# Attention, gated product and mixture of experts on one core: embedding norms, x scaling, filler banks and planner ranks rearranged

## The chip, the cores and the metric

One core of a Trainium2 chip runs the whole program in one launch. The metric is device time in microseconds (us) of that core; lower is better. The engines are PE (TensorE, matmuls and transposes), DVE (VectorE), ACT (ScalarE), POOL (GpSimd) and SP (SyncE, which here issues DMAs). Each engine works through its own instructions strictly in the order in which they were issued when the program was built.

## The reference

Three stages follow each other, cut here to what matters:

```python
scores = where(causal_mask, -1e9, q @ k.T / 8)        # 2 batches, 12 heads, 448 x 64
attn = exp(scores - max); attn /= attn.sum(-1) + 1e-9
x = (attn @ v) laid out as 896 tokens x 768
x = ((x @ w_a) * (x @ w_b)) @ w_out                   # 768 -> 1536 -> 768, float64 weights
xn = x / (norm(x) + 1e-6); en = expert_emb / (norm(expert_emb) + 1e-6)
expert = argmax(xn @ en.T / tau); gate = softmax(...)[expert]
out = gate * (relu(x @ w1[expert]) @ w2[expert])      # 8 experts, 768 -> 1024 -> 768
```

## The kernel before

**Attention.** Two heads make a pair; there are 12 pairs (6 a batch). A pair has three score units: the last 112 query rows, then the second 112, then the third and first together. Unit by unit, PE makes scores in PSUM (`scores`, L361, and the mask, L367), DVE takes the row extreme (`maxima`, L378), and ACT makes the exponentials (`exps`, L394). These are five sub-blocks of 112 x 448 a pair, 60 in all. Of each sub-block PE makes the transpose (`turn`, L403), ACT evacuates it to half precision (`p_hi`, L406), DVE makes the remainder (`p_lo`, L409), and PE multiplies with v in 12 small matmuls (`pv`, L425 to L427). At the pair's end DVE scales the context into x (`weigh`, L447). Four buffers each hold exponentials and transposed probabilities (NPB, NTB). Ahead of that, a pair's k is scaled by a constant (`k_scale`, L333: on DVE for the first pair, on POOL for the others), and v is scaled and split on POOL (L336, L340, L343). q, k and v come by SP's queue (`load`, L178).

**Between attention and the first product.** After a batch's last pair ACT sums squares of x (`squares`, L474), DVE makes a power of two per row (`norm`, L483 to L488), x is multiplied by it (`x_scale`, L493 on DVE and L495 on ACT), PE transposes it (`turn_x`, L461), and ACT and DVE split it into halves (`x_hi` L464, `x_lo` L468).

**First product.** w_a and w_b arrive as float64, and every 128-wide block is converted by DVE in four operations of 768 elements (`conv_ops`: a L258, b L262, c L266, d L273) with one on ACT (e, L269). A unit (f, hf) is two accumulations of 18 matmuls each (`mm`, L507, 128 x 448), followed by `g_a` (ACT), `g_b` (DVE), `g_hi` (ACT) and `g_lo` (DVE), L511 to L522. There are 24 units, 864 matmuls. Those of batch 0 (hf = 0, f = 0 to 3) may start while attention of batch 1 still runs, and fill PE's free time: they are the fillers. In that stretch PSUM holds two score tiles of two banks, two banks of transposes, one bank of context ("po") and one bank "ac" for the fillers.

**Expert embeddings.** 8 rows of 768 are loaded by POOL's queue (L226) into a part of gE, and DVE makes their norms in a chain of small operations (`emb_tasks`, L290 to L305). PE transposes them (`emb_turn`, L312), and ACT and DVE split them (L318, L321). They are first used in the second half of the first product (`we_mm`).

**What sets the order.** `Plan` is a list scheduler that runs while the program is built. Every operation is recorded with an engine, an estimated cost, what it depends on, and a rank. Among the operations that could start at once on the engine that is free first, the lowest rank is issued. So ranks and estimated costs fix each engine's sequence; on the chip the engines then wait for each other as real durations have it. Conversion n may start after exponentials number C1A + C1B*n (20, 25, ... 55).

Of the kernel before, what the change touches and what calls it, by code (L numbers as in the profile page):

```python
# [85 lines left out]
def fused_kernel(ctx: ExitStack, tc: tile.TileContext, q, k, v, w_a, w_b, w_out, emb, tau, w1, w2, out):  # L86
# [17 lines left out]
    NFIRST, NC1, C1A, C1B = 4, 8, 20, 5  # L104
# [118 lines left out]
    er = gE[:E].rearrange("e f h t -> e (f h t)").bitcast(F32)  # L223
    ej = er[:, DM : 2 * DM]
    er = er[:, :DM]
# [18 lines left out]
    def conv_ops(n, *dest_free, after=None):  # L244
# [45 lines left out]
        lambda: v_.scalar_tensor_tensor(ej, er, 1.0, er, op0=ALU.mult, op1=ALU.mult, accum_out=en),  # L290
# [207 lines left out]
    gt = {}  # L498
# [45 lines left out]
    TIE = {(0, 0): 0.45, (0, 1): 0.45, (1, None): 0.45, (2, 0): 0.45, (2, 1): 0.45}  # L544
# [4 lines left out]
    for pi, (b, hp) in enumerate(pairs):  # L549
# [55 lines left out]
    def unit(f, hf):  # L605
        ops_ = unit_o[f, hf] = []
        for i in range(2):
            for kc in range(KC):
                for n in range(3):
# [4 lines left out]
                    if first_:  # L614
                        deps += last(ac_free, pools["acs"])
# [7 lines left out]
        ac_free.append((gb,))  # L623
        gh = op("ACT", ACTC(S), lambda: g_hi(f, hf), gb, el, rank=501)
# [15 lines left out]
    plan.run([o for x in begun for o in unit_o[x]])  # L640
    prev_mm[0] = mm_o[begun[-1]] if begun else None
# [571 lines left out]
```

## Time and profile before

| | us |
|---|---|
| three runs: median (lowest to highest) | 584.49 (581.29 to 585.14) |
| the profiled execution's own time | 586.54 |
| its span, first to last instruction | 584.7 |
| PE busy in the span | 529.2 (90%) |
| DVE busy | 401.9 (69%) |
| ACT busy | 210.8 (36%) |
| POOL busy | 138.3 (24%) |

A busy share is an average over stages with different limits; the stretches below are read one by one. Matmuls are pipelined, so that a group's time is its end less its start, and the idle time ahead of an instruction stands in square brackets with the engine that ended it.

### The profile page before, as it was taken

What the parts mean: (1) busy time and instruction counts of PE and PEld (TensorE: products, weight loads), DVE (VectorE), ACT (ScalarE), POOL (GpSimd) and SP (SyncE); (2) the same over time, 40 slices, a digit from 0 to 9 for tenths busy, and PEclk for the clock granted to TensorE, in tenths of its full rate; (3) what the DMA queues carried; (4) which work ended last, traced back from release to release, by engine and by line L of the source; (5) the groups of instructions that cost most, each with busy time, mean ns of one, the idle gap of its engine ahead of it and who ended that gap; (6) DMA issues with size and microseconds to landing.
All of it is one profiled execution on the core that took longest, in us unless ns stands there. A gap on an engine that the chain in (4) does not pass through costs nothing. (4 is left out here: it accounts for less than half of the span.)

```text
span 584.7 us, 12576 instructions
## 1 busy us (share of the span) xinstructions
PE 529.2 (90%) x5094; PEld 356.6 (61%) x5094; DVE 401.9 (69%) x628; ACT 210.8 (36%) x487; POOL 138.3 (24%) x134
## 2 busy tenths in 40 slices
PE   0998879998999999999999999967999799999893
PEld 0676667664555555555466666657776768767682
DVE  3589989996799758997314788950989628678000
ACT  0687987894242222433201111122211332223230
POOL 7376655301000000000000000012333434324322
PEclk9999989999999999999999999979999899999998
DMA  6453441133546544698201689829788818756100
GB/s 197 142 164 97 151 144 59 56 109 84 188 131 197 176 143 127 144 261 227 55 1 57 229 286 319 290 84 134 233 251 280 289 49 282 246 196 193 44 15 33
DMA packets 46229, 93.02 MB, mean 159 GB/s; under 512 B 23430, under 2 KB 26502, under 8 KB 46160
## 3 DMA queue, kind: packets, MB, share of 16 engines
q1 hardware_dynamic: 43872, 84.16, 47.9%
q0 software_dynamic: 2288, 7.91, 3.8%
q8 instruction: 47, 0.77, 0.6%
q14 instruction: 22, 0.18, 0.1%
HBM read 79.46 MB, written 9.05 MB: 151 GB/s over the span
## 5 line engine op out<-in xcount | busy, mean ns | idle before, releaser
L507 PE MATMUL ab<-bufA 128*128 128x448 f16 x864 | 168.0, 352 | 2.4 <-ACT asb L511 1.8
L507 PEld LDWEIGHTS <-bufA 128*128 128x128 f16 x864 | 83.3, 98 | 77.5 <-issue 3.1
L893 PE MATMUL x<-woc,gL 128*128 128x512 f16 x336 | 57.9, 327 | 0.0
L983 POOL DMA_INDIRECT x<-xse,gidi x1 | 1.1, 1147 | 234.1 <-DVE bufB L876 234.1
L394 ACT ACTIVATE pr<-sc,mn 112x336 f32<-112x336 f32 (+2 forms) x96 | 46.4, 496 | 18.3 <-DVE mn L378 17.8
L361 PE MATMUL sc<-ld,ld 64*112 64x448 f32 (+3 forms) x192 | 34.8, 463 | 14.5 <-DVE ld L333 14.0
L893 PEld LDWEIGHTS <-gL 128*128 128x128 f16 x336 | 32.2, 98 | 20.6 <-issue 0.2
L1095 PEld LDWEIGHTS <-hh 128*128 128x128 f16 x320 | 30.9, 98 | 20.3 <-issue 0.4
L409 DVE TENSOR_TENSOR tbuf<-pt,tbuf 112x448 f16<-112x448 f32 x60 | 36.1, 618 | 4.6 <-ACT tbuf L406 4.5
L378 DVE TENSOR_REDUCE mn<-sc 112x2 f32<-112x896 f32 (+3 forms) x48 | 34.3, 734 | 5.6 <-PE sc L367 5.5
L1081 POOL TENSOR_TENSOR hl<-hr,hh 128x512 f16<-128x512 f32 x20 | 26.7, 1333 | 46.7 <-ACT hr L1080 38.8
L515 DVE TENSOR_TENSOR asb<-asb,ab 128x448 f32<-128x448 f32 x24 | 14.9, 619 | 32.8 <-PE ab L507 31.5
L406 ACT ACTIVATE tbuf<-pt 112x448 f16<-112x448 f32 x60 | 32.0, 544 | 13.8 <-PE pt L403 13.4
L1098 ACT ACTIVATE y<-py,sc 128x512 f32<-128x512 f32 (+1 forms) x20 | 10.5, 577 | 71.9 <-DMA sc<-xsc,gidi 27.0
L262 DVE SCALAR_TENSOR_TENSOR cv<-raw,cv 128x768 uint32<-128x768 uint32 x36 | 35.6, 989 | 1.1
L403 PE MATMUL pt<-id,pr 112*112 112x112 f32 x240 | 35.2, 273 | 0.1
L872 DVE TENSOR_SCALAR bufC<-rw 128x768 f16<-128x768 f32 (+1 forms) x28 | 20.0, 713 | 21.8 <-DMA rw<-in_moe_w_dram 15.6
L266 DVE SCALAR_TENSOR_TENSOR cv<-raw,cv 128x768 uint32<-128x768 uint32 x36 | 34.3, 952 | 0.5
L427 PE MATMUL po<-vh,tbuf 112*128 112x64 f16 x240 | 27.4, 194 | 7.9 <-DVE tbuf L409 7.9
L876 DVE SCALAR_TENSOR_TENSOR bufC<-rw,bufC 128x768 f16<-128x768 f32 (+1 forms) x28 | 32.6, 1163 | 1.4
L876 DVE SCALAR_TENSOR_TENSOR bufB<-rw,bufB 128x768 f16<-128x768 f32 (+1 forms) x28 | 32.4, 1158 | 1.3
L876 DVE SCALAR_TENSOR_TENSOR bufA<-rw,bufA 128x768 f16<-128x768 f32 (+1 forms) x28 | 30.0, 1073 | 1.3
(223 smaller groups left out, 1274.8 us busy)
## 6 DMA issues: line engine op xcount, KB each, us to landing
rw<-in_moe_w_dram SPq DMA_DIRECT2D x36, 512.0 KB, 5.4
rw<-in_moe_w_dram SPq DMA_DIRECT2D x48, 384.0 KB, 4.3
raw<-in_moe_w_a_dram SPq DMA_DIRECT2D x12, 768.0 KB, 4.3
raw<-in_moe_w_b_dram SPq DMA_DIRECT2D x12, 768.0 KB, 4.4
raw<-in_moe_w_out_dram SPq DMA_DIRECT2D x12, 768.0 KB, 5.1
ld<-in_k_dram SPq DMA_DIRECT2D x12, 224.0 KB, 2.8
ld<-in_q_dram SPq DMA_DIRECT2D x12, 224.0 KB, 3.5
ld<-in_v_dram SPq DMA_DIRECT2D x12, 224.0 KB, 3.5
```

The costliest lines, as they stand in the source:

```text
L262: nc.vector.scalar_tensor_tensor(t, r()[:, :, 1], 0xC0000000, t, op0=ALU.bitwise_and, op1=ALU.bitwise_or)
L266: nc.vector.scalar_tensor_tensor(t, r()[:, :, 0], 29, t, op0=ALU.logical_shift_right, op1=ALU.bitwise_or)
L361: nc.tensor.matmul(sc[:CP, j, o : o + W], qt[hd, c * CP : W], kt[hd, :W], start=n == 0, stop=False)
L378: nc.vector.tensor_reduce(mns[pi][:, c, :], sc[:CP, :, o : o + W], axis=AX.X, op=ALU.min)
L394: nc.scalar.activation(pr[:, d : d + W], sc[:CP, jj, o : o + W], AF.Exp, bias=mn[:, c, jj : jj + 1], scale=-1.0, accum_out=sums[pi][:, c, ...
L403: nc.tensor.transpose(pt[:CP, cs], prs[g][:, cs], id32[:CP, :CP])
L406: nc.scalar.activation(tbufs[g % NTB][:, 0, :S], pts[g][:CP, :S], AF.Copy)
L409: nc.vector.tensor_tensor(tbufs[g % NTB][:, 1, :S], pts.pop(g)[:CP, :S], tbufs[g % NTB][:, 0, :S], op=ALU.subtract)
L507: nc.tensor.matmul(gt[i][:, :S], w[:, h, i, kc, :], x[:, kc, ts], start=kc == n == 0, stop=kc == KC - 1 and n == 2)
L876: nc.vector.scalar_tensor_tensor(dl, R.pop(("raw", j, pc))[:, :n], SE, dh, op0=ALU.mult, op1=ALU.subtract)
L893: nc.tensor.matmul(xp[:, ns], G(f)[:, a, tk], woc[:, f, l, ns], start=st, stop=sp)
L1095: nc.tensor.matmul(py[:, ns], a[:, f, :], w_[:, f, ns], start=st, stop=sp)
```

## The change

1. The embeddings are loaded into x00, a tile used only much later, and their DVE, PE and ACT operations are recorded after attention with rank 400; the squares are written to a part of gL that is free until the end of the first product.
2. All four `x_scale` of a batch run on ACT.
3. The second accumulation of the filler units f = 1 to 3 goes to the bank "po", which is free after the last pair's `weigh`; the first stays in "ac".
4. The planner's ranks are new. Transposes and `p_hi` are drawn ahead of their sub-block (T and H), `pv` is put back (V), the units' scores are drawn apart (S), x transposes are drawn ahead (X). Conversion n may start after exponentials number 10 + 13n, at most the last (59).

```diff
-    NFIRST, NC1, C1A, C1B = 4, 8, 20, 5
+    NFIRST, NC1 = 4, 8
+    RK = dict(S=(-2.0, 5.0, -1.0), M=-1.2, T=-8.1, H=-6.8, L=0.0, V=2.7, sq=5.4, X=-9.5, C1A=10, C1B=13.0)
...
-    er = gE[:E].rearrange("e f h t -> e (f h t)").bitcast(F32)
-    ej = er[:, DM : 2 * DM]
-    er = er[:, :DM]
+    er = x00[:E]
     nc.gpsimd.dma_start(er, emb)
...
-        pte["t"] = pt = acc("pte")
+        pte["t"] = pt = small("pte")
...
-        if c % 2:
-            nc.vector.tensor_scalar(x0, x0, r2[b][:, c : c + 1], None, op0=ALU.mult)
-        else:
-            nc.scalar.activation(x0, x0, AF.Copy, scale=r2[b][:, c : c + 1])
+        nc.scalar.activation(x0, x0, AF.Copy, scale=r2[b][:, c : c + 1])
...
-            gt[i] = acc(f"ab{f}{i}{hf}")
+            gt[i] = psA.tile([P, 512], F32, tag="po", name=f"ab{f}{i}{hf}", bufs=1) if (f, hf, i) in on_po else acc(f"ab{f}{i}{hf}")
...
-    emb_o = None
-    for i, fn in enumerate(emb_tasks):
-        emb_o = op("DVE", 0.2, fn, emb_o, rank=12 + 0.01 * i)
-    eo = op("PE", 0.5, emb_turn, emb_o, rank=13)
-    eh = op("ACT", 0.3, emb_hi, eo, rank=13)
-    el = op("DVE", 0.25, emb_lo, eh, rank=13)
-    ac_free.append((el,))
...
-                t_o[g] = op("PE", 0.4, lambda g=g: turn(g), e_o[g], l_o.get(g - 2), rank=g + 0.5)
+                t_o[g] = op("PE", 0.4, lambda g=g: turn(g), e_o[g], l_o.get(g - 2), rank=g + RK["T"])
...
-        conv_ops(n, after=e_o[C1A + C1B * n])
+        conv_ops(n, after=e_o[min(int(RK["C1A"] + RK["C1B"] * n), NU - 1)])
+    po_free = [(wg_o[len(pairs) - 1],)]
     for f in range(NFIRST):
+        if f >= 1:
+            on_po.add((f, 0, 1))
         unit(f, 0)
...
+    eo = None
+    for i, fn in enumerate(emb_tasks):
+        eo = op("DVE", 1.7 if i == 0 else 0.18, fn, eo, rank=400)
+    eo = op("PE", 0.5, emb_turn, eo, rank=400)
+    eh = op("ACT", 0.3, emb_hi, eo, rank=400)
+    el = op("DVE", 0.25, emb_lo, eh, rank=400)
```

Three places show what moves. The changed kernel's lines stand one to four lower than those of the kernel before.

DVE at the program's start, before: the end of the embedding chain (esm holds its 8 norms, gE the embeddings), the first pair's k (ld), then the first row extremes (mn).

```order
L297 RECIPROCAL esm<-esm 8x1
L298 TENSOR_SCALAR esm<-esm 8x1
L299 TENSOR_SCALAR esm<-esm 8x1
L302 TENSOR_SCALAR esm<-esm 8x1
L303 RECIPROCAL esm<-esm 8x1
L333 TENSOR_SCALAR ld_0_84<-ld_0_84 128x448
L304 TENSOR_SCALAR gE<-gE,esm 8x768
L305 RECIPROCAL rtau<-rtau 128x1
L378 TENSOR_REDUCE mn_174<-sc_159 112x2
L378 TENSOR_REDUCE mn_174<-sc_169 112x2
```

The same place in the changed kernel, from DVE's first instruction:

```order
L188 CAST idb<-id_90 112x112
L190 CAST id_97<-id_90 128x128
L332 TENSOR_SCALAR ld_0_84<-ld_0_84 128x448
L377 TENSOR_REDUCE mn_157<-sc_142 112x2
L377 TENSOR_REDUCE mn_157<-sc_152 112x2
L408 TENSOR_TENSOR tbuf_107<-pt_173,tbuf_107 112x448
L377 TENSOR_REDUCE mn_157<-sc_186 112x2 x2
L408 TENSOR_TENSOR tbuf_109<-pt_181,tbuf_109 112x448
```

The first pair's k is the third instruction now; the embedding chain has gone from here.

DVE around batch 0's `norm` (n0sq), before: cv1 and cv2 are conversions 1 and 2, x0_0 is batch 0's x, tbuf the transposed probabilities.

```order
L409 TENSOR_TENSOR tbuf1_109<-pt29_1083,tbuf1_109 112x448
L266 SCALAR_TENSOR_TENSOR cv1_928<-raw1_263,cv1_928 128x768
L447 TENSOR_TENSOR x0_0_395<-po5_1016,rr5_1088 112x4x128
L258 TENSOR_SCALAR cv2_1150<-raw2_324 128x768
L262 SCALAR_TENSOR_TENSOR cv2_1150<-raw2_324,cv2_1150 128x768
L378 TENSOR_REDUCE mn6_1014<-sc62_1141 112x2 x2
L483 TENSOR_TENSOR n0sq_75<-nsq0_133 112x4
...
L488 TENSOR_SCALAR n0sq_75<-n0sq_75 112x4
L493 TENSOR_SCALAR x0_0_395<-x0_0_395,r20_135 112x768 x2
L409 TENSOR_TENSOR tbuf2_111<-pt30_1127,tbuf2_111 112x448
```

The same place in the changed kernel:

```order
L377 TENSOR_REDUCE mn6_999<-sc61_1037 112x2
L408 TENSOR_TENSOR tbuf1_109<-pt29_1045,tbuf1_109 112x448
L408 TENSOR_TENSOR tbuf2_111<-pt30_1071,tbuf2_111 112x448
L446 TENSOR_TENSOR x0_0_374<-po5_1001,rr5_1069 112x4x128
L482 TENSOR_TENSOR n0sq_75<-nsq0_133 112x4
...
L487 TENSOR_SCALAR n0sq_75<-n0sq_75 112x4
L408 TENSOR_TENSOR tbuf3_113<-pt31_1142,tbuf3_113 112x448
L377 TENSOR_REDUCE mn6_999<-sc62_1147 112x2 x2
```

The conversions have gone from around the norm, and sub-block 30's remainder stands ahead of it instead of behind it.

ACT behind the last pair, before: squares (junk), conversions (bufA from cv), x_scale of batch 1 (x0_1) and its evacuations (px).

```order
L474 ACTIVATE junk_132,nsq1_134<-x0_1_1358 112x640 x2
L518 ACTIVATE gE_79<-asb00_1927 128x448
L269 ACTIVATE bufA_74<-cv5_2030 128x768
L474 ACTIVATE junk_132,nsq1_134<-x0_1_1358 112x128 x4
L511 ACTIVATE asb10_2144<-ab100_2099 128x448
L269 ACTIVATE bufA_74<-cv6_2103 128x768
L495 ACTIVATE x0_1_1358<-x0_1_1358,r21_136 112x768 x2
L464 ACTIVATE bufA_74<-px10_2174 128x448 x2
```

The same place in the changed kernel:

```order
L473 ACTIVATE junk_132,nsq1_134<-x0_1_1294 112x640 x3
L514 ACTIVATE gE_79<-asb00_1854 128x448
L268 ACTIVATE bufA_74<-cv4_2031 128x768
L473 ACTIVATE junk_132,nsq1_134<-x0_1_1294 112x128 x4
L507 ACTIVATE asb10_2118<-ab100_2080 128x448
L491 ACTIVATE x0_1_1294<-x0_1_1294,r21_136 112x768 x4
L268 ACTIVATE bufA_74<-cv5_2104 128x768
L514 ACTIVATE gE_79<-asb10_2118 128x448
L463 ACTIVATE bufA_74<-px10_2155 128x448 x2
```

Four x_scale stand where two stood, and one conversion has moved behind them.

Counted in the two sequences of PE: ahead of the last `pv` matmul stand 39 filler matmuls before and 36 now; between it and the first x transpose of batch 1 stand 29 before and 42 now. The embeddings' transposes stand in the first product now, 41 filler matmuls behind the end of unit (2, 0). Counted in the two sequences of DVE: ahead of the last `weigh` (and behind the embedding chain) stand 7 conversion operations a, 7 b, 6 c and 5 d before, and 5, 5, 5 and 4 now; of conversion 0, a, b and c stand in the third and fourth pair now, in the fifth and sixth before.

## Rows read from the trace of the kernel before

**Rows 1.** Windows: stretch, length, busy us (instructions) of five engines, TensorE clock, DMA share, GB/s.

```profile
core 0: us, PE busy (x) PEld busy (x) DVE busy (x) ACT busy (x) POOL busy (x), PEclk, DMA share, GB/s
13.95:45.00 31.05, 30.11 (x349) 21.20 (x350) 21.77 (x38) 21.68 (x73) 16.99 (x18) 1.00 0.47 145
45.00:127.60 82.60, 74.72 (x976) 54.56 (x975) 79.58 (x136) 71.14 (x220) 40.28 (x37) 0.98 0.34 106
127.60:143.30 15.70, 12.57 (x77) 7.27 (x75) 13.34 (x25) 9.67 (x22) 2.18 (x2) 1.00 0.32 71
143.30:297.00 153.70, 151.82 (x928) 79.84 (x926) 115.60 (x157) 45.78 (x71) 0.00 (x0) 1.00 0.56 159
72.00:84.00 12.00, 8.74 (x106) 6.99 (x105) 10.42 (x23) 9.92 (x28) 4.49 (x3) 0.86 0.46 165
```

**Rows 2.** Timeline of the start: start us, duration us, engine, instruction [idle before, releaser].

```profile
0.81 0.40 SPq L178 DMA_DIRECT2D ld<-in_k_dram  x1
1.27 0.42 SPq L178 DMA_DIRECT2D ld<-in_q_dram  x1
...
9.03 1.70 DVE L290 SCALAR_TENSOR_TENSOR gE<-gE 8x768 f32<-8x768 f32 x1 [7.27 <-DMA gE<-in_moe_expert_emb_dram]
...
9.90 2.03 POOL L333 TENSOR_SCALAR ld<-ld 128x448 f32<-128x448 f32 x1
...
13.53 0.36 DVE L333 TENSOR_SCALAR ld<-ld 128x448 f32<-128x448 f32 x1
13.95 1.84 PE L361 MATMUL sc<-ld,ld 64*112 64x448 f32 x4 [13.95 <-DVE ld L333]
14.70 0.14 DVE L305 RECIPROCAL rtau<-rtau 128x1 f32<-128x1 f32 x1
17.47 0.80 PE L312 MATMUL pte<-id,gE 8*128 8x8 f32 x6
22.19 1.33 PE L361 MATMUL sc<-ld,ld 64*112 64x448 f32 x4
```

**Rows 3.** DMA issues of the first pair's k and q: KB, us from issue to landing.

```profile
ld<-in_k_dram SPq DMA_DIRECT2D x1, 224.0 KB, 2.7
ld<-in_q_dram SPq DMA_DIRECT2D x1, 224.0 KB, 2.8
```

**Rows 4.** Groups by line, DVE, 45 to 127.6 us: count, busy us, mean ns, idle before.

```profile
L262 DVE SCALAR_TENSOR_TENSOR cv<-raw,cv 128x768 uint32<-128x768 uint32 x7 | 7.8, 1117 | 0.2
L266 DVE SCALAR_TENSOR_TENSOR cv<-raw,cv 128x768 uint32<-128x768 uint32 x6 | 5.6, 936 | 0.0
L273 DVE SCALAR_TENSOR_TENSOR bufA<-cv,bufA 128x768 f16<-128x768 f32 x5 | 5.4, 1089 | 0.0
L258 DVE TENSOR_SCALAR cv<-raw 128x768 uint32<-128x768 uint32 x7 | 3.8, 541 | 0.0
L493 DVE TENSOR_SCALAR x<-x,r 112x768 f32<-112x768 f32 x2 | 1.1, 613 | 0.0
```

**Rows 5.** The same view, ACT, the same stretch: x_scale on ACT.

```profile
L495 ACT ACTIVATE x<-x,r 112x768 f32<-112x768 f32 x2 | 1.8, 928 | 0.0
```

**Rows 6.** Timeline around batch 0's norm: DVE's conversion b, POOL's v_lo, PE's pv.

```profile
70.59 1.80 DVE L262 SCALAR_TENSOR_TENSOR cv<-raw,cv 128x768 uint32<-128x768 uint32 x1
...
70.04 1.53 POOL L343 TENSOR_TENSOR vl<-ld,vh 112x512 f16<-112x512 f32 x1
...
75.98 0.20 PE L427 MATMUL po<-vh,tbuf 112*128 112x64 f16 x1 [3.26 <-DVE tbuf L409]
```

**Rows 7.** Waits, 45 to 127.6 us: who waited for whom, us in total, times, longest.

```profile
ACT tbuf L406 <- PE pt L403: 8.2, 11, 1.5
...
PE po L427 <- DVE tbuf L409: 7.1, 9, 3.3
```

**Rows 8.** Timeline of PE behind the last pair (fillers and x transposes).

```profile
126.68 3.00 PE L507 MATMUL ab<-bufA 128*128 128x448 f16 x15
130.59 2.81 PE L507 MATMUL ab<-bufA 128*128 128x448 f16 x14 [0.90 <-ACT asb L511]
133.23 1.70 PE L461 MATMUL px<-id,x 112*128 112x112 f32 x16
...
136.51 0.95 PE L461 MATMUL px<-id,x 112*128 112x112 f32 x8 [0.82 <-DVE bufA L468]
```

More of the change, by code (lines that the diff above doesn't have):

```diff
@@ L560, in fused_kernel @@
         vl_o[pi] = op("POOL", 1.2, lambda pi=pi: v_lo(pi), vh, rank=r0)
-        for u, rk in ((0, -3), (1, -1), (2, 1)):
+        for u, rk in enumerate(RK["S"]):
             sc_o[pi, u] = so = op("PE", SCOST[u], lambda pi=pi, u=u: scores(pi, u), k_o[pi], ld_[pi, 0],
                                   *last(sc_free, 2), rank=r0 + rk)
-            mx[pi, u] = op("DVE", 0.08 * len(UNITS[u]) + 0.00104 * 2 * W_(u), lambda pi=pi, u=u: maxima(pi, u), so, rank=r0 + rk)
+            mx[pi, u] = op("DVE", 0.08 * len(UNITS[u]) + 0.00104 * 2 * W_(u), lambda pi=pi, u=u: maxima(pi, u), so, rank=r0 + rk + RK["M"])
             mine = []
@@ L571, in fused_kernel @@
                 mine.append(e_o[g])
-                t_o[g] = op("PE", 0.4, lambda g=g: turn(g), e_o[g], l_o.get(g - 2), rank=g + 0.5)
-                h = op("ACT", ACTC(S), lambda g=g: p_hi(g), t_o[g], v_o.get(g - NTB), rank=g + 0.6)
-                l_o[g] = op("DVE", DVEC(S), lambda g=g: p_lo(g), h, rank=g + 0.6)
-                v_o[g] = op("PE", 0.37, lambda g=g: pv(g), l_o[g], vl_o[pi], wg_o.get(pi - 1), v_o.get(g - 1), rank=g + 1.5)
+                t_o[g] = op("PE", 0.4, lambda g=g: turn(g), e_o[g], l_o.get(g - 2), rank=g + RK["T"])
+                h = op("ACT", ACTC(S), lambda g=g: p_hi(g), t_o[g], v_o.get(g - NTB), rank=g + RK["H"])
+                l_o[g] = op("DVE", DVEC(S), lambda g=g: p_lo(g), h, rank=g + RK["L"])
+                v_o[g] = op("PE", 0.37, lambda g=g: pv(g), l_o[g], vl_o[pi], wg_o.get(pi - 1), v_o.get(g - 1), rank=g + RK["V"])
             sc_free.append(mine)
@@ L584, in fused_kernel @@
             sq_o[b, part, c] = op("ACT", ACTC(LATE if not part else DM - LATE) + 0.2, lambda b=b, c=c, part=part: squares(b, c, part),
-                                  wg_o[pi], rank=r0 + NSB + 5 - 6 * part)
+                                  wg_o[pi], rank=r0 + NSB + RK["sq"] - (RK["sq"] + 1) * part)
         if part == 0:
@@ L588, in fused_kernel @@
         no = op("DVE", 0.7, lambda b=b: norm(b), *(o for k, o in sq_o.items() if k[0] == b), rank=r0 + NSB)
-        xs_ = [op(("ACT", "DVE")[c % 2], (0.85, 0.6)[c % 2], lambda b=b, c=c: x_scale(b, c), no, rank=r0 + NSB + 0.1 * c) for c in range(NCH)]
+        xs_ = [op("ACT", 0.85, lambda b=b, c=c: x_scale(b, c), no, rank=r0 + NSB + 0.1 * c) for c in range(NCH)]
         for kc in range(KC):
             fr = last(ac_free, 1) if b == 0 else last(sc_free, 2) if kc % 2 == 0 else ()
-            to = op("PE", 0.4, lambda b=b, kc=kc: turn_x(b, kc), *xs_, *fr, x_o.get((b, kc - 1, "t")), rank=r0 + NSB + 3 + 0.1 * kc)
-            ho = op("ACT", ACTC(S), lambda b=b, kc=kc: x_hi(b, kc), to, rank=r0 + NSB + 3 + 0.1 * kc)
-            x_o[b, kc] = lo = op("DVE", DVEC(S), lambda b=b, kc=kc: x_lo(b, kc), ho, rank=r0 + NSB + 3 + 0.1 * kc)
+            to = op("PE", 0.4, lambda b=b, kc=kc: turn_x(b, kc), *xs_, *fr, x_o.get((b, kc - 1, "t")), rank=r0 + NSB + RK["X"] + 0.1 * kc)
+            ho = op("ACT", ACTC(S), lambda b=b, kc=kc: x_hi(b, kc), to, rank=r0 + NSB + RK["X"] + 0.1 * kc)
+            x_o[b, kc] = lo = op("DVE", DVEC(S), lambda b=b, kc=kc: x_lo(b, kc), ho, rank=r0 + NSB + RK["X"] + 0.1 * kc)
             x_o[b, kc, "t"] = to
@@ L614, in unit @@
                     if first_:
-                        deps += last(ac_free, pools["acs"])
+                        deps += last(po_free if (f, hf, i) in on_po else ac_free, pools["acs"])
                     prev_mm[0] = op("PE", 0.189, lambda f=f, hf=hf, i=i, kc=kc, n=n: mm(f, hf, i, kc, n), *deps, rank=5000)
@@ L622, in unit @@
         gb = op("DVE", DVEC(S), lambda: g_b(f, hf), prev_mm[0], ga, rank=500)
-        ac_free.append((gb,))
-        gh = op("ACT", ACTC(S), lambda: g_hi(f, hf), gb, el, rank=501)
+        (po_free if (f, hf, 1) in on_po else ac_free).append((gb,))
+        gh = op("ACT", ACTC(S), lambda: g_hi(f, hf), gb, rank=501)
         gl = op("DVE", DVEC(S), lambda: g_lo(f, hf), gh, rank=501)
@@ L640, in fused_kernel @@
     plan.run([o for x in begun for o in unit_o[x]])
+    on_po.clear()
     prev_mm[0] = mm_o[begun[-1]] if begun else None
```

7 lines of the change are left out of this document (3 added, 4 removed).

## Prediction

> **What bounds the kernel now.** I read the windows of the profile first, by stage [rows 1]. The reader is to see three different limits. Up to 13.95 us PE does nothing. From 45 to 127.6 us, most of attention, DVE is busy for 79.58 of 82.60 us (96%), ACT for 71.14 (86%) and PE for 74.72, so DVE sets the pace there; from 13.95 to 45 us DVE has 9.3 us to spare (21.77 of 31.05). From 143.3 to 297 us, the first product, PE is busy for 151.82 of 153.70 us, and DVE has 38 us to spare (115.60). What follows 297 us is not touched by the change and merely comes earlier or later. So a microsecond of DVE's work is worth most in attention and nothing in the first product, and the total is this: when PE gets its steady stream of first-product matmuls, less those already done as fillers.
>
> The start I read in the timeline [rows 2]. k and q of the first pair are issued at 0.81 and 1.27 us and land 2.7 and 2.8 us later [rows 3], so at 3.5 and 4.1 us. DVE, however, stands at the embeddings' first operation until 9.03 us, because their load lands only then (7.27 us of idle time, released by that DMA). The first pair's k_scale is queued behind the chain and runs at 13.53 us. PE's first score matmul follows at 13.95 us, released by it.
>
> **The change part by part.** The sum is made against the profiled execution, 586.54 us (span 584.7 and 1.8 around it). It lies 2.05 us above the median of the three runs; I carry the difference over to the median, 584.49.
>
> Start. In the changed order k_scale is DVE's third instruction. It needs 0.36 us from 3.5 us on; PE then waits for q, and begins at about 4.2 us instead of 13.95: 9.8 us gained. What is late next is POOL, which scales the second pair's k at 9.90 to 11.93 us [rows 2]. The second pair's scores came 8.2 us after the first pair's (22.19 less 13.95), so they would now be due at 12.4 us, after POOL is done. Bounds: 9.8 us if that margin of 0.5 us holds, nothing if POOL's chain sets the pace of the first pairs (a rival below). I take 9.8.
>
> DVE's load in attention. By the counts of the two sequences, two operations a, two b, one c and one d of the conversions leave attention: 2 x 0.541 + 2 x 1.117 + 0.936 + 1.089 = 5.3 us [rows 4]. Two x_scale of batch 0 go to ACT: 2 x 0.613 = 1.2 us less [rows 4]. And a, b, c of conversion 0 (2.6 us) move from the DVE-bound stretch into earlier pairs, where DVE had 9.3 us to spare. Together 9.1 us leave a stretch in which DVE had 3 us of idle time. They reappear in the first product, under 38 us of DVE's spare time, and cost nothing there; if that cover were gone, PE would wait for weights. Not all 9.1 us can be had: ACT gets two more x_scale (2 x 0.928 us [rows 5]), 73 us of work, and in 82.6 - 9.1 = 73.5 us it would have to be busy without a gap, while it now waits 8.2 us in that stretch for PE's transposes [rows 7]. Bounds 0 and 9.1; I take 5.0, a little over half, which leaves ACT at 94% in 77.6 us.
>
> At batch 0's norm the price can be seen. DVE has conversions ahead of and around the norm, one of them 1.80 us long instead of the mean 1.12 [rows 4, 6], and PE stands 3.26 us at a context matmul for DVE's remainder [rows 6]. That wait is part of the same 9.1 us and isn't counted again. The long one ran while POOL's v_lo took 1.53 us. The Trainium skill (SBUF — State Buffer, Who interferes with whom) says that a DVE instruction with two SBUF inputs and a GpSimd instruction that reads SBUF exclude each other for a whole instruction. The trace agrees with that at this place. It speaks against one edit: conversion 0, moved into earlier pairs, now meets POOL's work for the next pairs. By the rule three such blocks of up to 1 us could be added there and the gain be 12 us; by the row POOL is busy for 17 of 31 us in that stretch [rows 1] and can take them, and the sum stays as it is.
>
> Ranks. Transposes come further ahead of their context matmuls, so that p_hi and p_lo have longer before PE needs them. PE waited for DVE's remainder 7.1 us in nine places, ACT for transposes 8.2 us in eleven [rows 7]. In a stretch that DVE bounds these waits are its shadow; I count nothing, with bounds of 3 us either way (about half of either wait).
>
> Behind the last pair. Before, PE was busy 12.57 of 15.70 us [rows 1], 3.1 us of waits, such as 0.90 us for ACT to empty the single filler bank [rows 8]. With two banks those waits go. But x transposes of batch 1 come later: they began 6.55 us after the last context matmul (133.23 less 126.68 [rows 8]), and with four x_scale in a row on ACT instead of two beside two on DVE they need 2 x 0.928 = 1.9 us more, 8.4 us. PE has 42 fillers ahead of them instead of 29; at 0.19 us each (14 in 2.81 us, the last one's own 0.35 us taken off [rows 8]) that is 8.0 us, so 0.4 us stay uncovered. With some 0.7 us at the next group, 1.1 us of waits are left of 3.1: 2.0 us gained (bounds: 0 and 3.1).
>
> Fillers. 36 instead of 39 are done ahead of the last context matmul: 3 x 0.19 = 0.6 us lost.
>
> Embeddings. Their 0.80 us on PE [rows 2] now stand in the PE-bound product: 0.8 us lost at most. PE comes to them 41 x 0.19 = 7.8 us after the end of unit (2, 0). Behind that end DVE does g_b, a conversion d and g_lo (some 2.3 us) and the chain, 14.84 - 9.03 - 0.36 = 5.45 us [rows 2]: 7.8 us too. PE's wait is therefore between 0 and 1.5 us; I take 0.2, and 1.0 us for all.
>
> Sum: 9.8 + 5.0 + 2.0 - 0.6 - 1.0 = 15.2 us. The profiled execution would take 571.3 us, the median 569.3.
>
> **The rivals.** (a) Only the head is gained. ACT and PE, at 86% and 90% of the stretch already [rows 1], take over as soon as DVE is relieved, and the order's waits stay: 9.8 + 1.0 - 0.6 - 1.0 = 9.2 us, 575.3. For it: 73 us of ACT work cannot shrink. Against it: ACT's 86% contain 8.2 us of waits for PE, which itself waited for DVE.
>
> (b) Everything gives. The stretch loses all of 9.1 us, the tail all of 3.1, and the half-speed time at batch 0 goes too: from 72 to 84 us the granted clock is 0.86 [rows 1], which is 12 x 0.14 = 1.7 us of matmul time, and it follows the 3.26 us wait. The Trainium skill (TensorE: Matmul & The Clock Gate, Part 1) says that the slow clock is the default and activity releases it; the trace agrees, the low value standing at the longest wait of the stretch. Gain 9.8 + 9.1 + 3.1 + 1.7 - 0.6 - 0.8 = 22.3 us, 562.2. Against it: three engines would have to run without gaps together.
>
> (c) The change doesn't do at the start what it says: POOL, which scales k and splits v for the pairs to come, sets the pace of the first pairs, and the 9.8 us come back as waits for POOL. Gain 5.4 us, 579.1. For it: the margin of 0.5 us. Against it: POOL is busy 55% of 13.95 to 45 us.
>
> (d) Slower. Transposes drawn ahead stand in front of ready context matmuls, and PE, strictly in order, waits at each for ACT's exponentials, while ACT waits for PE. Such a wait took 8.2 / 11 = 0.75 us. At all 44 places of the stretch instead of 11 it would cost 33 x 0.75 = 25 us more, and the time would be 584.5 - 15.2 + 25 = 594. It decides from some 20 places more on. Against it: four buffers of exponentials let ACT run ahead of PE.
>
> **How the numbers follow.** The forecast, 566 to 573 us, has a chance of 0.56; (a) 0.18, (b) 0.15, (c) 0.07, (d) 0.04. About 1% is what a measurement of this kernel can tell from no change (its three runs span 0.7%), so faster means below 578.6 us: forecast, (a) and (b), 0.89. (c) lies within 1%: 0.07. Slower: 0.04. The range runs from 562 to 578 us; it leaves out (c), (d) and half of (b), 0.19 together.
>
> **What would show it.** The first score matmul at 4.2 us instead of 13.95, and the second pair's scores near 12.4 us (later, released by POOL: (c)). The last weigh at about 112.8 us instead of 127.6 (9.8 and 5.0 earlier): near 118 it is (a), near 109 (b). No wait of 3 us of PE at batch 0's norm. In the ten microseconds behind the last context matmul at most 1.5 us of PE waits, none of them for ACT's asb. The embeddings' transposes without a wait above 1.5 us. The first product as dense as before from its start on; PE waiting there for conversions would show that DVE's spare time was not where I put it. The forecast is wrong if the last weigh moves by less than 10 or more than 20 us, or if the stage behind 297 us changes its length.

## The result and the profile after

The changed kernel took 569.74 us (median of four runs, 563.65 to 573.23), the kernel before 584.80; the ratio is 0.9675 with a 95% interval of 0.960 to 0.975. Timed again later it took 566.93 us (565.66 to 568.14) against 584.08, ratio 0.9704 (0.967 to 0.974). The forecast was 569.3. Two of the four runs, the profiled one among them, are slow (573.07 and 573.23 us, over 1.5% above the fastest) and are left out of the ratio, which compares the other two (563.65 and 566.40) with the kernel before.

The profiled execution took 573.07 us (span 571.4). Its windows, with the columns of [rows 1]:

```profile
core 0: us, PE busy (x) PEld busy (x) DVE busy (x) ACT busy (x) POOL busy (x), PEclk, DMA share, GB/s
4.20:35.00 30.80, 28.39 (x329) 20.15 (x330) 22.20 (x38) 21.51 (x73) 23.04 (x23) 1.00 0.69 217
35.00:113.00 78.00, 72.83 (x961) 54.60 (x959) 68.98 (x123) 69.56 (x216) 36.04 (x38) 0.96 0.30 95
113.00:130.00 17.00, 16.73 (x121) 9.95 (x120) 16.04 (x29) 13.20 (x29) 1.91 (x2) 1.00 0.52 98
130.00:282.00 152.00, 149.78 (x919) 78.83 (x918) 120.79 (x178) 46.70 (x73) 0.00 (x0) 1.00 0.58 166
```

The stretch that was 45 to 127.6 us in [rows 1] is now 35 to 113 us, 4.6 us shorter; DVE is busy 88% of it instead of 96%, and behind the last pair PE hardly waits (16.73 of 17.00 us). The first product is as dense as before. The timeline of the start, to be held against [rows 2]:

```profile
3.47 0.40 DVE L332 TENSOR_SCALAR ld<-ld 128x448 f32<-128x448 f32 x1 [1.72 <-DMA ld<-in_k_dram]
4.13 1.84 PE L360 MATMUL sc<-ld,ld 64*112 64x448 f32 x4 [4.13 <-DMA ld<-in_q_dram]
...
9.45 1.33 POOL L332 TENSOR_SCALAR ld<-ld 128x448 f32<-128x448 f32 x1
...
12.06 1.01 PE L360 MATMUL sc<-ld,ld 64*112 64x448 f32 x4
```

The first scores wait for q alone, and POOL has the second pair's k ready at 10.78 us, 1.3 us ahead of its use. PE behind the last pair, to be held against [rows 8]:

```profile
113.81 8.11 PE L503 MATMUL ab<-bufA 128*128 128x448 f16 x42
121.75 1.70 PE L460 MATMUL px<-id,x 112*128 112x112 f32 x16
123.29 1.49 PE L503 MATMUL ab<-bufA 128*128 128x448 f16 x7
125.03 0.96 PE L460 MATMUL px<-id,x 112*128 112x112 f32 x8 [0.26 <-DVE bufA L467]
125.83 12.27 PE L503 MATMUL ab<-bufA 128*128 128x448 f16 x64
138.35 0.53 PE L311 MATMUL pte<-id,x 8*128 8x8 f32 x6 [0.25 <-DVE x L303]
```

42 fillers run without a gap up to the x transposes, no wait is for asb, and the embeddings' transposes cost 0.53 us and a wait of 0.25. The waits of attention (35.3 to 114.5 us), for [rows 7]:

```profile
ACT tbuf L405 <- PE pt L402: 3.6, 7, 0.9
...
PE po L426 <- DVE tbuf L408: 1.3, 1, 1.3
```

ACT's wait for transposes fell from 8.2 to 3.6 us, PE's for remainders from 7.1 to 1.3. The largest stall that is left is batch 0's join (56 to 72 us). There ACT makes six squares in a row, then four x_scale in two runs, and PE waits for the exponentials behind the squares:

```profile
59.14 0.31 ACT L473 ACTIVATE junk<-x 112x128 bf16<-112x128 f32 x1
...
60.21 0.99 PE L402 MATMUL pt<-id,pr 112*112 112x112 f32 x4 [2.07 <-ACT pr L393]
...
61.69 1.75 ACT L491 ACTIVATE x<-x,r 112x768 f32<-112x768 f32 x2
...
64.75 1.75 ACT L491 ACTIVATE x<-x,r 112x768 f32<-112x768 f32 x2
```

```profile
56.00:72.00 16.00, 11.50 (x123) 8.10 (x122) 7.87 (x19) 13.91 (x41) 6.01 (x6) 0.79 0.26 87
```

DVE is busy for half of these 16 us, ACT for 13.91, and PE's granted clock is 0.79. Before, DVE held the corresponding place [rows 6].

### The profile page after: what moved, and what is told of

It reads as the page before. It is cut to its first block, busy times and chain, and to the rows that moved or that the text cites. A ratio compares the mean times of both kernels' runs of the same rounds, so it can differ in the third digit from the quotient of the medians.

```text
span 571.4 us, 12592 instructions
## 1 busy us (share of the span) xinstructions
PE 527.4 (92%) x5094; PEld 357.4 (63%) x5094; DVE 396.5 (69%) x624; ACT 213.5 (37%) x491; POOL 130.7 (23%) x134
## 5 line engine op out<-in xcount | busy, mean ns | idle before, releaser
L393 ACT ACTIVATE pr<-sc,mn 112x336 f32<-112x336 f32 (+2 forms) x96 | 46.7, 500 | 12.4 <-DVE mn L377 12.4
L1079 POOL TENSOR_TENSOR hl<-hr,hh 128x512 f16<-128x512 f32 x20 | 25.5, 1274 | 50.5 <-ACT hr L1078 42.2
L874 DVE SCALAR_TENSOR_TENSOR bufA<-rw,bufA 128x768 f16<-128x768 f32 (+1 forms) x28 | 31.5, 1124 | 1.3
L511 DVE TENSOR_TENSOR asb<-asb,ab 128x448 f32<-128x448 f32 x24 | 14.8, 618 | 25.1 <-PE ab L503 24.9
L1077 ACT ACTIVATE hh<-ph 128x512 f16<-128x512 f32 x20 | 12.0, 599 | 49.7 <-PE ph L1071 49.6
```

The lines of the kernel that those rows point to most:

```text
L393: nc.scalar.activation(pr[:, d : d + W], sc[:CP, jj, o : o + W], AF.Exp, bias=mn[:, c, jj : jj + 1], scale=-1.0, accum_out=sums[pi][:, c, ...
L874: nc.vector.scalar_tensor_tensor(dl, R.pop(("raw", j, pc))[:, :n], SE, dh, op0=ALU.mult, op1=ALU.subtract)
```

## The experiments

All times of a stage are from the one profiled execution of each kernel; "first scores" and "last weigh" are starts; "fillers" are those ahead of the last context matmul; there is no E8; "behind" is from the product's end to the end of the span. Times and ratios come from four series, each with its own runs of the kernel before (median 584.54 us for E1 to E4; 584.08 for the changed kernel again, E5, E6 and E9; 584.68 for E7, E10 and E11; 585.18 for E12), and these alone differ by 1.1 us.

| kernel | first scores | last weigh | fillers | product's end | behind | median (lowest to highest) | ratio to before (95%) |
|---|---|---|---|---|---|---|---|
| before | 13.95 | 127.62 | 39 | 295.03 | 289.7 | 584.49 (581.29 to 585.14) | |
| changed | 4.13 | 114.54 | 36 | 280.35 | 291.0 | 569.74 (563.65 to 573.23) | 0.9675 (0.960 to 0.975) |
| changed, again | 4.21 | 113.47 | 36 | 279.16 | 285.0 | 566.93 (565.66 to 568.14) | 0.9704 (0.967 to 0.974) |
| E1 part 1 alone | 4.16 | 119.18 | 39 | 287.49 | 287.6 | 574.81 (573.26 to 576.82) | 0.9807 (0.975 to 0.986) |
| E2 part 1 undone | 13.39 | 121.76 | 36 | 287.71 | 288.4 | 577.03 (575.50 to 577.89) | 0.9845 (0.979 to 0.990) |
| E3 part 2 undone | 4.08 | 109.76 | 18 | 287.62 | 285.6 | 574.91 (574.86 to 578.04) | 0.9835 (0.977 to 0.990) |
| E4 part 3 undone | 4.06 | 114.71 | 36 | 282.34 | 287.1 | 569.24 (567.44 to 571.10) | 0.9710 (0.965 to 0.977) |
| E5 parts 1 to 3 | 4.19 | 121.59 | 49 | 284.71 | 285.1 | 572.07 (570.53 to 576.11) | 0.9798 (0.976 to 0.984) |
| E6 old conversion times alone | 4.13 | 113.19 | 36 | 278.21 | 287.7 | 567.36 (565.72 to 567.98) | 0.9703 (0.967 to 0.974) |
| E7 ranks T, H, L, V alone | 4.19 | 113.69 | 36 | 283.67 | 289.0 | 574.54 (574.18 to 584.88) | 0.9865 (0.981 to 0.992) |
| E9 old ranks, new conversion times | 5.00 | 119.61 | 46 | 284.71 | 287.6 | 572.03 (569.99 to 574.98) | 0.9791 (0.975 to 0.983) |
| E10 = E3 + second bank for all | 4.18 | 109.57 | 18 | 288.79 | 286.8 | 575.15 (570.38 to 577.30) | 0.9825 (0.977 to 0.988) |
| E11 join spread | 4.04 | 112.77 | 18 | 284.98 | 287.5 | 572.92 (571.24 to 574.25) | 0.9806 (0.977 to 0.985) |
| E12 = E10 + old conversion times | 4.86 | 113.35 | 18 | 284.88 | 286.9 | 573.98 (571.55 to 576.55) | 0.9799 (0.975 to 0.985) |

The stage behind the product differs between two executions of the changed kernel itself by 6 us, with the same work in it:

```profile
280.40:571.30 290.90, 261.22 (x2784) 194.73 (x2782) 168.64 (x258) 61.78 (x102) 66.23 (x53) 0.97 0.57 176
```

```profile
279.20:564.00 284.80, 257.81 (x2784) 191.31 (x2782) 168.34 (x258) 61.64 (x102) 66.98 (x53) 0.99 0.58 180
```

The granted clock is 0.97 in the one and 0.99 in the other. So the parts are compared by the product's end, and totals by medians. What was expected of the repetition:

> The changed kernel unaltered, once more, so that the variants beside it have a measure on the same chip. Expected: 569.7 us (563 to 573), last weigh at 114.5 us, the first product's end at 280.4, and the stage behind it 287 to 291 us long, which is where its own executions differ from each other.

**E1 and E2: the start.** E1 is the kernel before with the embeddings' lines of the change; E2 is the changed kernel without them. Two of those lines:

```diff
+    er = x00[:E]
...
+        eo = op("DVE", 1.7 if i == 0 else 0.18, fn, eo, rank=400)
```

> Only part 1 of the change, put into the kernel before: the embedding norms leave the start, everything else (order, ranks, banks, x_scale) stays. Theory: the start is worth its full 9.8 us less about 1.0 us for the embeddings' transposes in the first product, so the time is about 9 us (1.5%) below the kernel before, ratio 0.985; first score matmul at 4.1 us instead of 13.95 and the last weigh near 118 instead of 127.6. Rival 1 (POOL sets the pace of the first pairs): first score matmul at 4.1 us, but the last weigh only 3 to 6 us earlier, ratio 0.990 to 0.995. Rival 2 (all of the change's gain is the head, the rest is nothing): ratio 0.974, as the whole change has it.

> The changed kernel with part 1 undone: the embedding chain is back at the start, parts 2 to 4 stay. Theory: the parts are independent, so what is left is 13.1 less 9.8 = 3.3 us in attention and some 1.5 us behind it: first score matmul near 14 us, last weigh near 124.4, ratio to the kernel before 0.991 to 0.994 (579.5 to 581.5). Rival (the new ranks need the early start, or bring nothing without it): ratio 1.000 or above, last weigh at 127 or later.

E1 is 9.7 us faster than before (584.54 beside it), E2 7.5 us; together 17.2, which is what the whole change gives when it is timed again, in the next series (584.08 less 566.93). So the two halves add up, and both rivals of E1 fall. E2's last weigh came 5.9 us earlier, more than expected; 0.6 of that is an earlier first score. In E1 the 9.8 us of the first score had become 8.4 at the last weigh: the lead was 9.45 us at the first pair's weigh, 9.1 at the third's, 8.4 at the seventh's, behind the join.

**E3 and E10: x_scale split again.** E3 undoes part 2:

```diff
-        nc.scalar.activation(x0, x0, AF.Copy, scale=r2[b][:, c : c + 1])
+        if c % 2:
+            nc.vector.tensor_scalar(x0, x0, r2[b][:, c : c + 1], None, op0=ALU.mult)
+        else:
+            nc.scalar.activation(x0, x0, AF.Copy, scale=r2[b][:, c : c + 1])
...
+        xs_ = [op(("ACT", "DVE")[c % 2], (0.85, 0.6)[c % 2], lambda b=b, c=c: x_scale(b, c), no, rank=r0 + NSB + 0.1 * c) for c in range(NCH)]
```

> The changed kernel with part 2 undone: x_scale split between ACT and DVE again. In the changed kernel DVE is busy 88% and ACT 89% of attention, and at batch 0's join (pairs 6 to 8) ACT works without a gap at squares and x_scale while PE waits. Theory A (ACT bounds that join and the four x_scale lengthen it): last weigh 1 to 2 us earlier than 114.5, x transposes of batch 1 begin 6.5 us behind the last context matmul instead of 8.15, first product at most 0.4 us earlier for that since fillers cover it; time 0.5 to 2 us below the changed kernel (ratio to it 0.996 to 0.999). Theory B (DVE still bounds): last weigh 1 us later, ratio to the changed kernel 1.001 to 1.003.

Both theories missed. The last weigh came 4.8 us earlier, but the planner now put 18 fillers ahead of it instead of 36 (18 x 0.19 = 3.4 us of PE's time), and behind it the product took far longer. Two rows of the timeline, and the window around the first:

```profile
112.98 6.21 PE L506 MATMUL ab<-bufA 128*128 128x448 f16 x17 [3.48 <-ACT asb L510]
119.03 1.70 PE L460 MATMUL px<-id,x 112*128 112x112 f32 x16
```

```profile
109.00:119.00 10.00, 6.48 (x27) 2.90 (x28) 8.80 (x16) 6.86 (x18) 1.19 (x1) 0.66 0.48 158
```

With 18 fillers done, the next accumulation is due just where ACT makes squares, and asb stands behind seven of them (not nine, as I wrote for E10). PE waits 3.48 us, and the 17 matmuls behind that wait take 6.21 us instead of 3.4, at a granted clock of 0.66. E10 takes that wait away:

```diff
-        if f >= 1:
+        if f >= 0:
             on_po.add((f, 0, 1))
```

> The variant with x_scale split between ACT and DVE, which took 574.9 us, with one thing more: unit (0, 0)'s second accumulation goes to the bank po too, so that no filler behind the last context matmul needs ACT to have emptied ac. In the split variant PE stood 3.48 us there for asb, which ACT could make only behind nine squares, and the 17 fillers behind that wait took 6.21 us instead of 3.3. Theory (that wait and the half clock behind it made the split variant slow, not the split): the wait goes, the last weigh stays at 109.8 us, the product ends at 279 to 282 instead of 287.6, the time is 565 to 569. Rival (fewer fillers ahead, 18 instead of 36, make it slow): the product still ends at 285 or later, time 572 or more.

The wait went (1.00 us for the last weigh is left there, at full clock behind it), and the product still ended at 288.8 us. A later wait took its place:

```profile
110.31 5.65 PE L506 MATMUL ab<-bufA 128*128 128x448 f16 x29 [1.00 <-DVE x L446]
...
130.92 0.53 PE L311 MATMUL pte<-id,x 8*128 8x8 f32 x6 [0.48 <-DVE x L303]
134.77 0.55 PE L506 MATMUL ab<-bufA 128*128 128x448 f16 x2 [3.32 <-ACT bufA L268]
136.23 14.01 PE L506 MATMUL ab<-bufA 128*128 128x448 f16 x58 [0.90 <-DVE bufA L272]
```

```profile
135.00:142.00 7.00, 6.10 (x18) 2.41 (x17) 6.89 (x10) 0.84 (x1) 0.00 (x0) 0.52 0.69 238
```

A conversion isn't ready when the fourth unit needs it, and nearly 7 us at the lower of the two clocks follow, 1.2 GHz (0.52 of full speed granted). My rival (fewer fillers) gave the right time, but not by its own mechanism. On DVE that conversion's b and c stand right behind the embeddings' chain, which runs from 126.42 to 130.93 us:

```profile
126.42 0.94 DVE L289 SCALAR_TENSOR_TENSOR gL<-x 8x768 f32<-8x768 f32 x1
...
130.79 0.14 DVE L304 RECIPROCAL rtau<-rtau 128x1 f32<-128x1 f32 x1
...
131.38 0.94 DVE L261 SCALAR_TENSOR_TENSOR cv<-raw,cv 128x768 uint32<-128x768 uint32 x1
...
132.90 0.94 DVE L265 SCALAR_TENSOR_TENSOR cv<-raw,cv 128x768 uint32<-128x768 uint32 x1
```

**E12: is that the conversions put off, or the embeddings' chain?** E10 with the old times of the conversions:

```diff
-    ... C1A=10, C1B=13.0)
+    ... C1A=20, C1B=5.0)
```

> The variant with the split x_scale and two banks for all second accumulations (575.2 us, the first product's end at 288.8 us in its profile) with the old times of the conversions (number n after exponentials 20 + 5n) as its only edit. That variant had the last weigh at 109.6 us, but PE stood 3.32 us in the product for a conversion's ACT part at 134.8 us and 0.9 us for its DVE part, and ran at half clock behind it (granted clock 0.52 from 135 to 142 us); when attention ended it had done 4, 4, 4 and 3 of the four DVE operations of the conversions, and this order has 6, 6, 5 and 4. Theory D (conversions that are put off from attention are a debt on DVE, due when the first units of batch 0 need them): the wait at 134.8 us and the half clock behind it go, the last weigh is at 109.5 to 111.5 us, the product ends at 280 to 283 us, the time is 566 to 570 us. Rival E (the embeddings' 4.5 us chain on DVE, which stands ahead of that conversion, is what PE waits for): a wait of 2 to 4 us stays within 10 us of the embeddings' transposes, the product ends at 285 us or later, the time is 572 us or more.

```profile
117.00:145.00 28.00, 28.00 (x164) 15.63 (x163) 25.73 (x53) 10.06 (x18) 2.17 (x2) 1.00 0.40 126
```

PE worked without any gap from 117 to 145 us at full clock, with the embeddings' chain still on DVE (131.0 to 135.5 us): as theory D said, the wait goes when the conversions come earlier, and the chain by itself doesn't make it. That the chain had no part in E10's wait isn't shown: its 4.5 us stood right ahead of the late conversion there, and the two waits are 4.2 us together; no run took it away. The product still ended at 284.9 us instead of 280 to 283. The last weigh moved from 109.6 to 113.4 us, with 18.9 us of DVE's conversions ahead of it instead of 12.7, and PE then waited for it, with the lower clock behind (26 matmuls at full clock take some 5.1 us):

```profile
114.09 6.56 PE L506 MATMUL ab<-bufA 128*128 128x448 f16 x26 [1.59 <-DVE x L446]
```

The time stayed (ratio to E10, which is of another series, 0.999, 0.994 to 1.005), as rival E had it, though not by its mechanism. Here the debt was paid in attention instead of in the product.

**E4: one bank.**

```diff
-        if f >= 1:
-            on_po.add((f, 0, 1))
```

> The changed kernel with part 3 undone: all fillers in the one bank ac. Theory: behind the last context matmul PE waits again for ACT to empty the bank, about 0.9 us for each of the two or three accumulations that are done there ahead of the x transposes, so PE is busy some 14 to 15 of 17 us instead of 16.7 of 17, and the end of the first product stands 1.5 to 3 us later against the last weigh (166.75 + 2 between the last context matmul and the product's end); ratio to the changed kernel 1.003 to 1.005. Rival (the second bank is worth nothing, since x transposes would have come no earlier): PE waits more there, but the end of the first product moves by under 0.5 us; ratio 1.000.

```profile
118.17 3.56 PE L503 MATMUL ab<-bufA 128*128 128x448 f16 x18 [0.63 <-ACT asb L507]
...
128.95 10.94 PE L503 MATMUL ab<-bufA 128*128 128x448 f16 x57 [0.63 <-ACT asb L507]
```

The waits for asb are back, 0.63 us each rather than 0.9, and from the last context matmul to the product's end it is 168.6 us instead of 166.7: 1.8 us, as the theory had it. Its median lies between the two medians of the changed kernel, so the total doesn't show it.

**E5, E6, E9: ranks or conversions?** The changed kernel with the old ranks and old conversion times (E5), the old conversion times alone (E6), the old ranks alone (E9):

```diff
-    RK = dict(S=(-2.0, 5.0, -1.0), M=-1.2, T=-8.1, H=-6.8, L=0.0, V=2.7, sq=5.4, X=-9.5, C1A=10, C1B=13.0)
+    RK = dict(S=(-3.0, -1.0, 1.0), M=0.0, T=0.5, H=0.6, L=0.6, V=1.5, sq=5.0, X=3.0, C1A=20, C1B=5.0)
```

> Parts 1 to 3 of the change alone: the planner's old ranks and the old times of the conversions (number n after exponentials 20 + 5n). In this order 49 filler matmuls stand ahead of the last context matmul instead of 36. Theory L (DVE's load makes attention's gain): DVE has 5.3 us of conversions more in attention than the changed kernel, so the last weigh is at 117 to 119 us instead of 114.5; the 13 extra fillers (13 x 0.19 = 2.5 us) come back in a shorter product, 164 to 165 us from the last context matmul instead of 166.75. Net 0 to 2 us slower than the changed kernel (ratio 1.000 to 1.004). Theory R (the ranks make it): the same last weigh, so this run alone doesn't tell L from R; the two beside it do.

> The changed kernel with the old times of the conversions only; the new ranks stay, and 36 fillers stand ahead of the last context matmul as in the changed kernel. Theory L (DVE's load): the conversions are back in attention (5.3 us of DVE), so the last weigh is at 117 to 119.5 us instead of 114.5 and the end of the first product 3 to 5 us later; ratio to the changed kernel 1.005 to 1.009. Theory R (the ranks, by spacing transposes and context matmuls): the last weigh stays at 114.5 to 115.5 us and the time is within 1 us of the changed kernel's.

> The changed kernel with the old ranks; conversions late (10 + 13n) as in the changed kernel. 46 fillers stand ahead of the last context matmul instead of 36 (10 x 0.19 = 1.9 us of the product done earlier, if PE has the room). Theory L (DVE's load): the last weigh at 114 to 116 us as in the changed kernel, and the product's end the same or up to 2 us earlier: the ranks are worth nothing or less. Theory R (the ranks): the last weigh at 117 to 119 us, and the time 2 to 4 us above the changed kernel's.

Against the changed kernel beside them E5 takes 1.010 of its time (1.006 to 1.014), E9 1.010 (1.006 to 1.013), E6 1.000 (0.998 to 1.003). The conversion times make no difference to the time under either set of ranks; the ranks make 5.1 us with the new conversion times (E9) and 4.7 with the old (E5 against E6). Theory L is out, theory R stands. With the old ranks the last weigh does come 2.0 us earlier when the conversions are put off (E9 against E5; 3 fillers fewer are 0.6 of that), but the product's end doesn't move: PE waits longer behind attention, 1.84 us of it for a transposed block of w_out at 258.34 us. The windows of attention of the changed kernel (again) and of E6:

```profile
35.00:113.50 78.50, 73.28 (x974) 54.87 (x971) 69.78 (x125) 70.37 (x219) 35.16 (x37) 0.96 0.29 93
```

```profile
35.00:113.20 78.20, 73.82 (x968) 54.95 (x965) 75.26 (x130) 70.98 (x220) 36.69 (x38) 0.96 0.32 103
```

E6 gives DVE 5.5 us more to do in the same 78 us, and it is busy for 96% of them instead of 89%, the share that I had read as a bound in [rows 1]. The waits tell the sides apart; E5 (36 to 121.6 us), then E6 (35 to 113.2):

```profile
ACT tbuf L405 <- PE pt L402: 7.9, 13, 1.5
...
PE po L426 <- DVE tbuf L408: 4.0, 7, 1.0
```

```profile
ACT tbuf L405 <- PE pt L402: 2.4, 8, 0.6
...
PE po L426 <- DVE tbuf L408: 0.2, 1, 0.2
```

With old ranks PE reaches a context matmul before DVE has its remainder, and ACT reaches p_hi before PE has made the transpose; with the new ones the first wait is nearly gone and the second less than a third, although DVE has nearly as much to do (75.3 us instead of 78.3). E9, with the old ranks and the conversions out of the way, still has 7.4 and 3.2 us of them (35 to 119.6 us).

**E7: which ranks?** The changed kernel with the old S, M, sq and X.

```diff
+    RK = dict(S=(-3.0, -1.0, 1.0), M=0.0, T=-8.1, H=-6.8, L=0.0, V=2.7, sq=5.0, X=3.0, C1A=10, C1B=13.0)
```

> The changed kernel with the new ranks of transposes, p_hi, p_lo and context matmuls alone (T, H, L, V); the ranks of scores, row extremes, squares and x transposes (S, M, sq, X) are the old ones again. 36 fillers stand ahead of the last context matmul, as in the changed kernel. Theory R1 (the gain of the ranks, 5.1 us between the variant with all old ranks and the changed kernel, is that of transposes drawn ahead of their context matmuls): last weigh at 113 to 115 us, the product's end at 278 to 281, the time within 1 us of the changed kernel's. Rival R2 (drawing scores, squares and x transposes apart at batch 0's join makes it): last weigh at 117 to 120 us, the time 3 to 5 us above the changed kernel's.

The last weigh is at 113.69 us: for attention T, H, L and V are enough (R1). But the time is 7.6 us above the changed kernel's, which neither theory had. Behind the last pair:

```profile
130.44 3.20 PE L503 MATMUL ab<-bufA 128*128 128x448 f16 x16 [0.72 <-DVE bufA L272]
136.74 0.53 PE L311 MATMUL pte<-id,x 8*128 8x8 f32 x6 [3.10 <-DVE x L303]
```

```profile
136.00:145.00 9.00, 8.26 (x39) 4.10 (x40) 7.92 (x14) 0.79 (x2) 0.00 (x0) 0.81 0.29 92
```

In this order PE comes to the embeddings' transposes 3.10 us ahead of DVE's chain, and a lower clock follows. The product ends 4.5 us later than in the changed kernel (283.67 less 279.16); the rest of the 7.6 lies in the stage behind it (289.0 us against 285.0), whose length varies between executions of one kernel too.

**E11: an attempt at the join.** New ranks for batch 0, and the second bank for all fillers as in E10:

```diff
+ rank=r0 + NSB + (RK["sq"] - (RK["sq"] + 1) * part if b else 5.4 + 0.6 * part)   # squares
+ rank=r0 + NSB + (0.1 * c if b else 7 + 1.2 * c)                                # x_scale
+ rank=r0 + NSB + (RK["X"] + 0.1 * kc if b else 11 + 0.9 * kc)                   # x transposes
```

> An attempt to better the changed kernel at batch 0's join, where pairs 6 to 8 take 25.5 us for two pairs that take some 15 elsewhere: batch 0's squares, x_scale and x transposes are given ranks spread over the next pairs instead of coming in a row, so that ACT can make exponentials and p_hi between them; all second accumulations of the fillers use the bank po, as 18 fillers stand ahead of the last context matmul here and 35 behind it. Theory (ACT's run of squares and x_scale holds PE at the join): two pairs there take 16 to 20 us, the last weigh comes at 105 to 108.5 us (of which 18 x 0.19 = 3.4 us are fillers done later), and the time is 2 to 6 us below the changed kernel's, 561 to 565. Rival (the work is merely spread, all engines being near 90% busy): the last weigh at 109.5 to 111 us, and the time within 1 us of the changed kernel's.

From first score to first score, the two pairs at the join took 21.5 us instead of 25.1, but the following two lost it again (21.3 instead of 17.2), the last weigh came at 112.77 us with 18 fillers fewer ahead of it, and the time is 6 us above the changed kernel's. Both were wrong; the rival's reason is nearer. Behind the last pair PE waits for the last weigh, since the bank po isn't free, and 35 fillers take 8.47 us instead of some 6.8:

```profile
113.51 8.47 PE L503 MATMUL ab<-bufA 128*128 128x448 f16 x35 [1.00 <-DVE x L446]
```

```profile
112.30:122.00 9.70, 8.70 (x45) 4.21 (x42) 8.20 (x16) 7.83 (x18) 0.92 (x1) 0.82 0.50 163
```

No kernel tried is measurably faster than the changed one.

## Why the prediction came out right, point by point

The total was right, and of its largest two terms one was right in size and cause; the other came out in size by luck, since something else that had been set at nothing gave as much. That the first median (569.74) lies 0.4 us from the forecast is luck too, for none of the four runs lies within 2 us of it; timed again, the gain is 17.2 us instead of 15.2. Read at the product's end, the steps are 7.5 us for the start (E1 against before), 2.8 for parts 2 and 3 (E5 against E1) and 5.5 for the ranks (the changed kernel, again, against E5), 15.9 in all; by medians 9.7, 2.7 and 5.1 (E1 is of another series than E5).

- **Start, 9.8 us.** Right at its place: 4.13 us instead of the forecast 4.2, the second pair at 12.06 instead of 12.4. POOL's margin was 1.3 us, so rival (c) falls. In attention 1.4 us of the lead were lost again (E1), which the sum didn't have.
- **DVE's load in attention, 5.0 us.** The amount came (4.6 us between E1's last weigh and the changed kernel's), the cause was wrong. The step that failed is "DVE sets the pace there", read from a busy share of 96%, and with it "In a stretch that DVE bounds these waits are its shadow; I count nothing" for the ranks. Put back, the conversions cost 0.4 us by the medians (E6); the ranks, set at 0 with bounds of 3 us, gave 5.1. Where x_scale is split, putting them back does cost 3.8 us of attention (E10, E12), and with the old ranks 2.0 (E9, E5), though neither shows in the time, so DVE isn't far from being the bound, but it wasn't the one that the change removed. The Trainium skill (Perfetto Trace Analysis, Identifying the Most-Contended Engine) says that the engine with the highest occupancy is the one to relieve first. The runs here differ: once the order kept PE and ACT from waiting for each other, attention took the same time with DVE at 89% and, given 5.5 us more to do, at 96% (E6).
- **"cost nothing there", of the conversions put off.** True within 0.7 us in the changed kernel (166.6 us from the last context matmul to the product's end, 166.0 in E6), but the cover isn't DVE's 38 spare microseconds of the whole product: in E10 PE waited 3.32 us at 134.8 us for one of them. What counts is what is ready when the fourth unit of batch 0 begins.
- **Two instructions against POOL.** Conversion 0's a, b and c took 0.51, 0.95 and 0.95 us in the early pairs, so that meeting POOL cost DVE nothing, as the row had it (POOL's k_scale beside a and b took 1.77 us instead of 1.33); beside POOL's v_lo a conversion d took 1.24 us (at 93.03 us).
- **Behind the last pair, 2.0 us.** PE waited 0.3 us (forecast 1.1), x transposes came 8.15 us behind the last context matmul (forecast 8.4); from there to the product's end it is 166.7 us instead of 168.4 with 3 fillers more to do, so 2.2 us, of which E4 shows 1.8 to be the bank's. The 166.7 us hold the embeddings as well, 0.9 us by the next point; without them the term is 3.1 us, the upper bound.
- **Fillers 0.6, embeddings 1.0 us.** The product of E1, with the embeddings in it and nothing else changed, is 0.9 us longer (169.3 against 168.4).
- **Rivals.** (a) needed the last weigh near 118 us, (b) near 109: it was 114.5 and 113.5. But half of what (a) argued did show: with the order's waits left as they were, DVE's relief brought no time (E9 against E5). (d), transposes in the way of context matmuls, has its sign wrong: drawing them and p_hi ahead and putting pv back, together, is what gave attention its 5 us (E7).
- **The stage behind the product** changed its length, from 289.7 to 291.0 and 285.0 us. I had named that as a sign against me; it is what the changed kernel does from execution to execution, at clocks of 0.97 and 0.99.

Open: PE's waits for remainders, 4.0 us in E5 and 1.3 in the changed kernel, are half of what the ranks gave; the rest isn't assigned to single waits. Which of T, H, L and V does it wasn't tried one by one. What part 2 is worth by itself wasn't found, since undoing it makes the planner order everything else anew.

## What to carry to other kernels

A high busy share is no proof of a bound: put the engine's work back and see whether the end moves, and look first at the waits of the others, which an order of issue can remove without less work. Work that is put off is due somewhere, as the conversions in E10 and the embeddings' chain in E7 were; look for the instruction that needs it, not for the spare time of the whole stage. With a list scheduler, undoing one part can reorder all others (E3 has 18 fillers instead of 36), so count what stands ahead of the end of each stage before comparing times.

## What the runs showed of the hardware that was not expected

A wait of some 3 us on PE was followed by a loss of half to four fifths of its length again. In E3 3.48 us were followed by 17 matmuls that took 2.8 us too long; in E10 3.32 and 0.90 us by 7 us at a granted clock of 0.52 (7 x 0.48 = 3.4 us lost); in E7 3.10 us by 9 us at 0.81 (1.7 us). Behind E4's waits of 0.63 us the next 18 matmuls took 3.56 us, the time they take at full clock. The length of the one wait doesn't settle it: behind 1.00 us in E10 29 matmuls took 5.65 us, full speed, and behind 1.00 us in E11 35 took 8.47 us, some 1.7 too long. The Trainium skill (TensorE: Matmul & The Clock Gate, HAM oscillation — how this bites in real kernels) tells of the same pattern, a wait after which the next block starts slow; the rows on E3, E7 and E10 agree and give its price here.

DVE and POOL can lengthen each other: conversion b takes 0.95 us alone, but 1.80 us beside POOL's v_lo [rows 6], which took 1.53 us instead of 1.16, in the kernel before and again in E1. Overlap alone doesn't do it: at 67.14 us of the kernel before a conversion b overlapped POOL's v_scale by 0.56 us, and neither took longer than elsewhere (0.95 and 1.49 us).
